# Four parts of w_in ahead of the attention loop, between the first loads

## The chip, the core and the metric

The kernel runs on one NeuronCore of a Trainium2 chip. The metric is the time of one execution in device microseconds (us). Its engines are TensorE (PE, with its weight loads listed as PEld), VectorE (DVE), ScalarE (ACT) and GpSimd (POOL); SyncE (SP) issues nearly all transfers. Each engine runs its own instructions strictly in order and waits on semaphores for the others.

## What is computed

Three stages follow each other. The first is attention over 512 local positions with a window of 32 either way, plus 32 global positions, for 4 batches and 8 heads of 64. The second is a dense feed-forward layer on its 2,176 tokens, and the third a routed layer of eight experts.

```
x = attention(q_l, k_l, v_l, q_g, k_g, v_g)            # 2176 x 512
h = x @ w_in                                           # 512 -> 2048
g = max(h, 0) + alpha * min(h, 0)
y = g @ w_out                                          # 2048 -> 512
# then each token goes to one of 8 experts with 272 places each, the largest
# gate logits y @ w_gate first; out = max(y @ w1[e], 0) @ w2[e]
```

## The kernel before

**Attention** works on 16 units (a batch and two heads), two units to a *pair*: 8 pairs. `load(p)` (lines 323 to 335) issues a pair's loads, one transfer for queries and keys (`qk`, line 332) and one for values (`v`, line 335) per unit. The first pair's `qk` comes in two cuts, one of 416 columns and one of 1,024, so that products can start early. There are four `qk` and four `v` buffers, two pairs' worth. A pair has four *blocks* of 128 queries: scores on PE (line 366), mask and maximum on DVE (372), four exps on ACT (374), `norm` on DVE (379, 380, and four multiplications at 386), transposes (392, copied by ACT at 394), and products with the values (403, copied by ACT at 405). The global queries of a pair add lines 419 to 454. `attention()` is a generator; each `next` writes out a piece of this.

**Weights** `w_in` and `w_out` come in eight-byte floats and are worked out on the chip in *parts*: eight of `w_in` (`win_part`, parts 0 to 7) and eight of `w_out` (`wout_part`) for the first half of the hidden columns. `decode` (75 to 89) loads a part of 512 KB with a transfer on SP into `raw` (line 79, three buffers), takes the absolute value on ACT into `mag` (line 82, two buffers), and assembles the float in four steps on DVE (lines 83, 85, 86, 87). `split` (71 to 73) then casts the high part on ACT (line 72) and subtracts it for the low part on POOL (line 73).

**The dense layer** goes over the tokens in column blocks of 272; its first product (`gemm1`, line 172) needs `w_in`'s parts, its leaky relu is an ACT step (177) and a DVE step that writes `g` (178), `g` is split (ACT and POOL, `ghi` and `glo`), and the second product (line 203) needs `w_out`'s parts. A first column block cannot be finished before the last part of `w_out` is there.

**Order.** Up to line 527, attention runs alone, until the first two pairs are done (`done[0]`), and after every sixth piece one of `w_in`'s parts 0 to 3 is written out. Lines 528 to 530 load `alpha` and the gate weights `wg`. Then a loop mixes attention with the dense layer and writes out one of the remaining twelve parts at each step of the latter, none of them issued ahead of the second pair's last norm. What the program writes out is reordered per engine by a scheduler before it runs, so the place in the code isn't the place in the queue: parts 0 to 3 stand in the queues behind much of the first pair.

Of the kernel before, what the change touches and what calls it, by code (L numbers as in the profile page):

```python
# [25 lines left out]
def tile_attention_moe_moe(ctx: ExitStack, tc: tile.TileContext, qkw, vw,  # L26
# [5 lines left out]
    E, _, FF = w1.shape  # L32
# [4 lines left out]
    KD = DM // 128  # L37
# [14 lines left out]
    def kpos(i):  # L52
        return WIN * (i + (i + 1) // 2)
# [17 lines left out]
    def split(hi, lo, src, lo_eng=None):  # L71
        a = A.copy(hi, src)  # L72
        return a, (lo_eng or V).tensor_tensor(lo, src, hi.bitcast(F32), op=OP.subtract)  # L73
# [3 lines left out]
    def decode(pool, src, n):  # L77
        raw = pool.tile([128, n, 2], I32, name="raw", bufs=RB[0])
        nc.sync.dma_start(out=raw.rearrange("p n t -> p (n t)"), in_=src)
        low, high = raw[:, :, 0], raw[:, :, 1]  # L80
        mag = pool.tile([128, n], F32, name="mag", bufs=2)
        A.activation(out=mag, in_=high.bitcast(F32), func=AF.Abs)
        V.tensor_scalar(mag, mag, F64_MIN, None, op0=OP.max)
        bits = mag.bitcast(I32)
        V.tensor_scalar(bits, bits, 3, 0x3FFFFFF8, op0=OP.logical_shift_left, op1=OP.bitwise_and)
        V.scalar_tensor_tensor(bits, high, -0x40000000, bits, op0=OP.bitwise_and, op1=OP.bitwise_or)
        V.scalar_tensor_tensor(bits, low, 29, bits, op0=OP.logical_shift_right, op1=OP.bitwise_or)
        return mag
# [11 lines left out]
    def win_part(pool, hf, i):  # L100
        c, k = divmod(i, KD)
        o = hf * HF + c * 512
        val = decode(pool, w_in.bitcast(I32)[k * 128:(k + 1) * 128, 2 * o:2 * o + 1024], 512)
        split(WI[hf][:, 0, k, c * 512:(c + 1) * 512], WI[hf][:, 1, k, c * 512:(c + 1) * 512], val, lo_eng=P)
# [185 lines left out]
    with ExitStack() as at:  # L290
# [5 lines left out]
        dc = at.enter_context(tc.tile_pool(name="dc", bufs=1, side="right"))  # L296
# [23 lines left out]
        QS = 4 * WIN  # L320
        STEPS = S // QS

        def load(p):
            for cut in range(2 if p == 0 else 1):
                for u in (2 * p, 2 * p + 1):
                    d = U[u]
                    if not cut:
                        d["qk"] = ld.tile([128, S + KL + 2 * SG], F32, name="qk")
                        d["k"] = d["qk"][:, QS:QS + KL]
                        d["g"] = d["qk"][:, S + KL:]  # L330
                    part = slice(None) if p else (slice(0, QS + kpos(6)), slice(QS + kpos(6), None))[cut]
                    nc.sync.dma_start(out=d["qk"][:, part], in_=qkw[u, :, part])
            for u in (2 * p, 2 * p + 1):
                U[u]["v"] = ld.tile([128, NQ, 2 * D], F32, name="vv")
                nc.sync.dma_start(out=U[u]["v"].rearrange("p i d -> p (i d)"), in_=vw[u])
# [131 lines left out]
        def attention():  # L467
            todo = []

            def one():  # L470
                if todo:
                    x, f = todo.pop(0)
                    f()
                    yield x

            N = STEPS * NU // 2
            for n in range(N + 2):
                p, j = divmod(n, STEPS)
                if n < N:
                    if j == 0 and 2 * p + 2 < NU:  # L480
                        load(p + 1)
                    scores(p, j)
                    yield 0.75
                if 1 <= n <= N:
                    a_ = divmod(n - 1, STEPS)
                    norm(*a_)
                    ptrans(*a_)
                    yield 0.45
                yield from one()
                if n >= 2:  # L490
                    v, j2 = divmod(n - 2, STEPS)
                    pv(v, j2)
                    yield 1.0
                    if j2 == STEPS - 1:
                        gout(v)
                        yield 0.1
                if n < N and j == 0:
                    todo += [(0.8, lambda p=p: (gscores(p, 0), gscores(p, 1))), (0.0, lambda p=p: gnorm(p)),
                             (0.6, lambda p=p: (gtrans(p, 0), gtrans(p, 1))), (1.2, lambda p=p: gpv(p))]

        load(0)
        mask = mk.tile([128, 3, KW], F32, name="mask")
        P.memset(mask, 0.0)
        for h in range(4):
# [11 lines left out]
        gpat = mk.tile([128, KL], F32, name="gpat")  # L516
        P.memset(gpat, 0.0)
        UPB = H // 2
        parts = [(win_part, i) for i in range(2 * KD)]
        att = attention()  # L520
        n = 0
        while done[0] < UPB - 1:
            next(att)
            n += 1
            if n >= 6 and n % 6 == 0 and len(parts) > KD:
                f, i = parts.pop(0)
                f(dc, 0, i)
        nc.sync.dma_start(out=al, in_=alpha.rearrange("(f p) -> p f", p=128))
        V.tensor_scalar(al1, al, -1.0, 1.0, op0=OP.mult, op1=OP.add)
        nc.sync.dma_start(out=wg[:, :, :E], in_=w_gate.rearrange("(k p) e -> p k e", p=128))  # L530
# [11 lines left out]
        while going:  # L542
# [12 lines left out]
            else:  # L555
# [4 lines left out]
                else:  # L560
                    spent["g"] += x
                    if parts:
                        f, i = parts.pop(0)
# [7 lines left out]
    with tc.tile_pool(name="dc2", bufs=1, side="right") as dc, tc.tile_pool(name="pW", bufs=2, space=PSUM) as pW:  # L571
        more = []
        parts = [(win_part, i) for i in range(2 * KD)] + [(wout_part, i) for i in range(KH)]
        n = 0
        while c < NCH:
# [4 lines left out]
            while next(g, None) is not None:  # L580
                n += 1
                if n % 5 == 0 and parts:
                    f, i = parts.pop(0)
# [13 lines left out]
    with ExitStack() as mo:  # L597
# [592 lines left out]
        for k in range(E):  # L1190
            n = 0.0
# [94 lines left out]
```

## Time and profile before

| | |
|---|---|
| median of 3 runs | 869.96 us (869.75 to 871.96) |
| profiled execution | 870.56 us, its span 868.8 us |
| mean granted clock of PE | 0.978 of full speed |
| PE busy | 820.1 us, 94% of the span |
| DVE busy | 466.8 us, 54% |
| ACT busy | 389.6 us, 45% |
| POOL busy | 348.5 us, 40% |

The span is the stretch from the first to the last instruction on the core; the execution's time has some 1.8 us around it. The shares are means over the whole span; the rows further down take it apart by stretch. In a row of the timeline, the first number is the start in us from the span's beginning, the second the time to the end of the last of the instructions that it groups (x4 stands for four in a row); brackets hold the engine's idle time just before and what released it. "PEclk" is PE's granted clock, where 1.00 stands for 2.4 GHz and 0.50 for 1.2.

### The profile page before, as it was taken

What the parts mean: (1) busy time and instruction counts of PE and PEld (TensorE: products, weight loads), DVE (VectorE), ACT (ScalarE), POOL (GpSimd) and SP (SyncE); (2) the same over time, 40 slices, a digit from 0 to 9 for tenths busy, and PEclk for the clock granted to TensorE, in tenths of its full rate; (3) what the DMA queues carried; (4) which work ended last, traced back from release to release, by engine and by line L of the source; (5) the groups of instructions that cost most, each with busy time, mean ns of one, the idle gap of its engine ahead of it and who ended that gap; (6) DMA issues with size and microseconds to landing.
All of it is one profiled execution on the core that took longest, in us unless ns stands there. A gap on an engine that the chain in (4) does not pass through costs nothing. (4 is left out here: it accounts for less than half of the span.)

```text
span 868.8 us, 21017 instructions
## 1 busy us (share of the span) xinstructions
PE 820.1 (94%) x8380; PEld 746.0 (86%) x8380; DVE 466.8 (54%) x1654; ACT 389.6 (45%) x970; POOL 348.5 (40%) x300
## 2 busy tenths in 40 slices
PE   6699799999988999999999999999899999999995
PEld 4478688888988999988898899999699989999995
DVE  4789945463288734133333457666575776722120
ACT  5577646464454543232322434341254535444431
POOL 1214412020145534200000638470598868779601
PEclk9589999999999999999999999999999999999998
DMA  9777715631345302201311217242366655666300
GB/s 345 230 255 272 261 38 192 212 124 47 95 134 183 114 26 79 72 7 53 103 52 54 78 54 267 64 131 65 100 198 217 168 177 153 174 187 185 111 25 37
DMA packets 50441, 115.94 MB, mean 133 GB/s; under 512 B 6759, under 2 KB 23399, under 8 KB 48295
## 3 DMA queue, kind: packets, MB, share of 16 engines
q1 hardware_dynamic: 47447, 105.68, 37.8%
q0 software_dynamic: 2896, 8.92, 3.1%
q8 instruction: 66, 1.08, 0.5%
q14 instruction: 32, 0.26, 0.1%
HBM read 96.76 MB, written 17.83 MB: 132 GB/s over the span
## 5 line engine op out<-in xcount | busy, mean ns | idle before, releaser
L172 PE MATMUL h<-xh,win 128*128 128x272 f32 x768 | 162.3, 295 | 3.9 <-DVE g L178 2.5
L73 POOL TENSOR_TENSOR m<-raw,m 128x1024 fp32r<-128x1024 f32 x64 | 152.4, 2402 | 21.6 <-ACT m L72 21.3
L172 PEld LDWEIGHTS h<-xh,win 128*128 128x128 f32 x768 | 124.9, 188 | 12.0 <-issue 4.9
L73 POOL TENSOR_TENSOR glo<-g,ghi 128x272 fp32r<-128x272 f32 x64 | 55.4, 866 | 150.8 <-ACT ghi L72 150.7
L203 PE MATMUL y<-ghi,wout 128*128 128x272 f32 x512 | 112.5, 298 | 2.5 <-ACT wout L72 1.3
L172 PE MATMUL h<-xl,win 128*128 128x272 f32 x384 | 111.3, 290 | 1.4 <-DVE xl L73 1.4
L1104 PE MATMUL h<-gr,wout 128*128 128x272 f32 x768 | 110.7, 295 | 0.0
L73 POOL TENSOR_TENSOR gr<-gb,gr 128x272 fp32r<-128x272 f32 x64 | 48.0, 772 | 153.2 <-ACT gr L72 144.6
L977 PE MATMUL h<-xsh,m 128*128 128x272 f32 x512 | 107.4, 297 | 1.3 <-ACT xsh L72 1.3
L993 PE MATMUL h<-hh,m 128*128 128x272 f32 x512 | 103.2, 293 | 0.0
L1104 PEld LDWEIGHTS h<-gr,wout 128*128 128x128 f32 x768 | 99.2, 188 | 0.9 <-ACT gr L72 0.4
L203 PEld LDWEIGHTS y<-ghi,wout 128*128 128x128 f32 x512 | 84.3, 188 | 8.3 <-issue 4.0
L177 ACT ACTIVATE neg<-h 128x272 f32<-128x272 f32 x128 | 50.5, 395 | 90.1 <-PE h L172 89.7
L977 PEld LDWEIGHTS h<-xsh,m 128*128 128x128 f32 x512 | 83.1, 190 | 1.9 <-ACT xsh L72 1.4
L993 PEld LDWEIGHTS h<-hh,m 128*128 128x128 f32 x512 | 81.7, 188 | 0.7 <-issue 0.5
L72 ACT CAST m<-raw 128x1024 fp32r<-128x1024 f32 x64 | 65.4, 1049 | 29.1 <-DMA raw<-in_moe_w_dram 28.9
L993 PE MATMUL h<-hl,m 128*128 128x272 f32 x256 | 75.5, 295 | 0.0
L203 PE MATMUL y<-glo,wout 128*128 128x272 f32 x256 | 73.8, 293 | 1.8 <-POOL glo L73 1.5
L977 PE MATMUL h<-xsl,m 128*128 128x272 f32 x256 | 74.9, 292 | 0.5 <-DVE xsl L73 0.5
L172 PEld LDWEIGHTS h<-xl,win 128*128 128x128 f32 x384 | 72.3, 188 | 2.4 <-DVE xl L73 1.9
L178 DVE SCALAR_TENSOR_TENSOR gb<-neg,al,h 128x272 f32<-128x272 f32 x64 | 31.6, 496 | 76.5 <-ACT neg L177 66.0
L374 ACT ACTIVATE pr<-sc,mx 128x128 f32<-128x128 f32 x128 | 50.1, 393 | 30.6 <-DVE mx L372 30.4
(231 smaller groups left out, 1517.2 us busy)
## 6 DMA issues: line engine op xcount, KB each, us to landing
raw<-in_moe_w_dram SPq DMA_DIRECT2D x64, 512.0 KB, 3.8
vv<-in_v_dram SPq DMA_DIRECT2D x16, 1024.0 KB, 8.0
qk<-in_qk_dram SPq DMA_DIRECT2D x14, 720.0 KB, 8.5
raw<-in_moe_w_in_dram SPq DMA_DIRECT2D x16, 512.0 KB, 4.4
raw<-in_moe_w_out_dram SPq DMA_DIRECT2D x16, 512.0 KB, 4.2
xs<-xb SPq DMA_DIRECT2D x16, 272.0 KB, 8.8
xpart<-xd SPq DMA_DIRECT2D x32, 136.0 KB, 1.7
xb<-xs SPq DMA_DIRECT2D x8, 544.0 KB, 4.0
```

The costliest lines, as they stand in the source:

```text
L72: a = A.copy(hi, src)
L73: return a, (lo_eng or V).tensor_tensor(lo, src, hi.bitcast(F32), op=OP.subtract)
L172: T.matmul(ps, wi[:, w, k, fs], x[:, k], start=i == 0, stop=i == 3 * KD - 1)
L177: A.activation(out=neg, in_=ps, func=AF.Relu, scale=-1.0)
L178: epi[0] = V.scalar_tensor_tensor(g, neg, al1[:, hf * KH + f:hf * KH + f + 1], ps, op0=OP.mult, op1=OP.add)
L203: T.matmul(ps, wo[:, w, f, ds_], x[:, f], start=i == 0, stop=i == 3 * KH - 1)
L374: A.activation(out=d["pr", j][:, ii], in_=sc, func=AF.Exp, bias=d["mx", j][:, ii:ii + 1], scale=-1.0, accum_out=d["sm", j][:, ii:ii + 1])
L977: T.matmul(ps, d["w1"][:, w, kk, fs], x[:, kk], start=i == 0, stop=i == 3 * KD - 1)
L993: T.matmul(ps, d["w2"][:, w, f, ms], x[:, f], start=i == 0, stop=i == 3 * K3 - 1)
L1104: T.matmul(ps[j], wo[:, w, f, ds_], x, start=f == 0 and a == 0, stop=f == KH - 1 and a == 2)
```

## The change

Parts 0 to 3 of `w_in` are no longer written out by the loop of lines 519 to 527 but inside the first `load`: parts 0 and 1 behind the first cuts of `qk`, parts 2 and 3 behind the second cuts, ahead of the values. Whatever belongs to a part (its transfer, ACT, DVE and POOL instructions) is written out there. The remaining parts keep their places in the code.

```
-        def load(p):
+        def load(p, between=()):
             for cut in range(2 if p == 0 else 1):
                 for u in (2 * p, 2 * p + 1):
...
                     nc.sync.dma_start(out=d["qk"][:, part], in_=qkw[u, :, part])
+                for f in between[2 * cut:2 * cut + 2]:
+                    f()
...
-        load(0)
+        parts = [(win_part, i) for i in range(2 * KD)]
+        load(0, [lambda i=i: win_part(dc, 0, i) for _, i in parts[:KD]])
+        del parts[:KD]
...
-        parts = [(win_part, i) for i in range(2 * KD)]
         att = attention()
-        n = 0
         while done[0] < UPB - 1:
             next(att)
-            n += 1
-            if n >= 6 and n % 6 == 0 and len(parts) > KD:
-                f, i = parts.pop(0)
-                f(dc, 0, i)
```

What the scheduler makes of it is seen in the engines' queues. In the following rows the line numbers after the change are two higher inside `load` from the values on and in attention, and two lower behind the loop.

SyncE's queue from its first transfer, before (`qk` and `vv` are attention's loads, `raw` a part, `al` and `wg` the alpha and the gate weights; x2 is one for each unit of a pair):

```order
L332 DMA qk<-in_qk_dram 128x416 x2
L332 DMA qk<-in_qk_dram 128x1024 x2
L335 DMA vv<-in_v_dram 128x2048 x2
L332 DMA qk<-in_qk_dram 128x1440 x2
L335 DMA vv<-in_v_dram 128x2048 x2
L79 DMA raw<-in_moe_w_in_dram 128x1024 x3
L528 DMA al<-in_moe_alpha_dram 128x16x1
L530 DMA wg<-in_moe_w_gate_dram 128x4x8
```

The same queue after:

```order
L332 DMA qk<-in_qk_dram 128x416 x2
L79 DMA raw<-in_moe_w_in_dram 128x1024 x2
L332 DMA qk<-in_qk_dram 128x1024 x2
L79 DMA raw<-in_moe_w_in_dram 128x1024
L337 DMA vv<-in_v_dram 128x2048 x2
L332 DMA qk<-in_qk_dram 128x1440 x2
L337 DMA vv<-in_v_dram 128x2048 x2
L526 DMA al<-in_moe_alpha_dram 128x16x1
L528 DMA wg<-in_moe_w_gate_dram 128x4x8
L79 DMA raw<-in_moe_w_in_dram 128x1024 x3
```

Two parts now stand ahead of the first pair's second cuts and one behind them; the fourth needs a `raw` buffer that the first has left, and it stands behind the gate weights.

ACT's queue before, from its second row (`pr` exps, `pt` and `gt` copies of transposes, `gsc` the global exps, `xb` the output copies, `mag` a part's absolute value):

```order
L374 ACTIVATE pr,sm<-sc,mx 128x128 x8
L394 COPY pt<-t 128x512
L424 ACTIVATE gsc,gmx<-gsc,gmx 128x544
...
L443 COPY gt<-gt 128x512
L374 ACTIVATE pr,sm<-sc,mx 128x128
L82 ACTIVATE mag<-raw 128x512
```

And after, its first rows, then the fourth part and what stands around it:

```order
L82 ACTIVATE mag<-raw 128x512
L376 ACTIVATE pr,sm<-sc,mx 128x128 x4
L82 ACTIVATE mag<-raw 128x512
L72 CAST win<-mag 128x512
...
L376 ACTIVATE pr,sm<-sc,mx 128x128 x4
L82 ACTIVATE mag<-raw 128x512
L407 COPY xb<-o 128x2x128
L396 COPY pt<-t 128x512
L82 ACTIVATE mag<-raw 128x512
L72 CAST win<-mag 128x512
L82 ACTIVATE mag<-raw 128x512
L407 COPY xb<-o 128x2x128
```

The first part's absolute value is now ACT's first instruction, and the fourth to sixth stand between the exps of the second pair's first and second blocks.

GpSimd's queue from the first subtract on, before (`win` and `wout` are the low parts of weights, `glo` that of one leaky relu):

```order
L73 TENSOR_TENSOR win<-mag,win 128x512 x8
L73 TENSOR_TENSOR glo<-g,ghi 128x272 x3
L73 TENSOR_TENSOR wout<-mag,wout 128x512
L73 TENSOR_TENSOR glo<-g,ghi 128x272
L73 TENSOR_TENSOR wout<-mag,wout 128x512
L73 TENSOR_TENSOR glo<-g,ghi 128x272 x2
L73 TENSOR_TENSOR wout<-mag,wout 128x512
L73 TENSOR_TENSOR glo<-g,ghi 128x272
```

And after:

```order
L73 TENSOR_TENSOR win<-mag,win 128x512 x8
L73 TENSOR_TENSOR wout<-mag,wout 128x512 x2
L73 TENSOR_TENSOR glo<-g,ghi 128x272
L73 TENSOR_TENSOR wout<-mag,wout 128x512 x2
L73 TENSOR_TENSOR glo<-g,ghi 128x272 x2
L73 TENSOR_TENSOR wout<-mag,wout 128x512
L73 TENSOR_TENSOR glo<-g,ghi 128x272
L73 TENSOR_TENSOR wout<-mag,wout 128x512
```

The parts of `w_out` have moved ahead against the leaky relus: before, two stand ahead of the sixth `glo`, after, seven.

## Rows read from the trace of the kernel before

**Rows 1.** Busy us by stretch: start:end and length first, (x) instructions, clock, DMA
```profile
core 0: us, PE busy (x) PEld busy (x) DVE busy (x) ACT busy (x) POOL busy (x), PEclk, DMA share, GB/s
5.10:24.50 19.40, 15.88 (x274) 10.37 (x274) 11.02 (x73) 10.08 (x41) 0.00 (x0) 1.00 1.01 403
24.50:39.70 15.20, 7.43 (x104) 4.38 (x105) 12.40 (x31) 8.27 (x20) 3.81 (x3) 0.54 0.71 217
39.70:50.50 10.80, 10.70 (x160) 7.80 (x160) 6.35 (x39) 8.45 (x32) 1.26 (x1) 0.54 0.84 268
50.50:85.20 34.70, 32.34 (x565) 26.53 (x548) 33.58 (x116) 26.24 (x83) 12.75 (x11) 1.00 0.74 264
85.20:112.00 26.80, 21.52 (x293) 17.43 (x297) 26.15 (x77) 17.93 (x51) 11.09 (x9) 1.00 0.62 215
112.00:200.00 88.00, 88.00 (x1411) 76.82 (x1398) 45.77 (x230) 50.96 (x179) 13.99 (x17) 1.00 0.40 139
```

**Rows 2.** Timeline at 25 us: start, duration, engine, line, op, [idle before <-releaser]
```profile
24.56 0.66 ACT L82 ACTIVATE mag<-raw 128x512 f32<-128x512 f32 x1 [2.19 <-DMA raw<-in_moe_w_in_dram]
27.23 1.92 PE L403 MATMUL o<-pt,vv 128*64 128x32 f32 x32 [2.78 <-ACT xb L405]
28.02 0.62 ACT L72 CAST win<-mag 128x512 fp32r<-128x512 f32 x1 [0.84 <-DVE mag L87]
```

**Rows 3.** Busy times of a short stretch, columns as in rows 1
```profile
48.00:50.00 2.00, 2.00 (x20) 0.85 (x24) 0.02 (x1) 1.17 (x4) 0.00 (x0) 0.60 0.89 254
```

**Rows 4.** SyncE's queue, timeline: start of issue, time held
```profile
7.49 4.14 SPq L79 DMA_DIRECT2D raw<-in_moe_w_in_dram  x3
16.62 10.20 SPq L530 DMA_DIRECT2D wg<-in_moe_w_gate_dram  x1
```

**Rows 5.** Issue to landing, line 79's transfers up to 130 us
```profile
DMA to landing us min/median/max: 3.5/4.5/17.0
```

**Rows 6.** Timeline before 46 us: first exp, waiting product, two norms
```profile
5.41 0.40 ACT L374 ACTIVATE pr<-sc,mx 128x128 f32<-128x128 f32 x1 [3.38 <-DVE mx L372]
7.52 0.65 PE L366 MATMUL s<-qk 64*32 64x128 f32 x8 [2.59 <-DMA qk<-in_qk_dram]
28.38 1.90 DVE L386 TENSOR_SCALAR pr<-pr,sm 128x128 f32<-128x128 f32 x4
41.99 0.87 DVE L386 TENSOR_SCALAR pr<-pr,sm 128x128 f32<-128x128 f32 x4
```

**Rows 7.** Timeline of VectorE: two steps of a decode without company
```profile
25.71 0.43 DVE L85 TENSOR_SCALAR mag<-mag 128x512 int32<-128x512 int32 x1
26.17 0.69 DVE L86 SCALAR_TENSOR_TENSOR mag<-raw,mag 128x512 int32<-128x512 int32 x1
```

**Rows 8.** VectorE's groups, 50.5 to 85.3 us: xcount | busy us, mean ns
```profile
L386 DVE TENSOR_SCALAR pr<-pr,sm 128x128 f32<-128x128 f32 x18 | 6.1, 393 | 0.1
L86 DVE SCALAR_TENSOR_TENSOR mag<-raw,mag 128x512 int32<-128x512 int32 x7 | 5.9, 865 | 0.0
L87 DVE SCALAR_TENSOR_TENSOR mag<-raw,mag 128x512 int32<-128x512 int32 x7 | 4.7, 677 | 0.0
L85 DVE TENSOR_SCALAR mag<-mag 128x512 int32<-128x512 int32 x7 | 4.6, 684 | 0.1
L83 DVE TENSOR_SCALAR mag<-mag 128x512 f32<-128x512 f32 x7 | 2.8, 420 | 0.4 <-ACT mag L82 0.4
```

**Rows 9.** Timeline at 78 us: GpSimd's subtract beside a decode step
```profile
77.44 1.27 POOL L73 TENSOR_TENSOR wout<-mag,wout 128x512 fp32r<-128x512 f32 x1 [0.54 <-ACT wout L72]
77.74 1.52 DVE L86 SCALAR_TENSOR_TENSOR mag<-raw,mag 128x512 int32<-128x512 int32 x1
```

**Rows 10.** Timeline: the three marks of the reckoning
```profile
50.54 0.29 DVE L372 CUSTOM_DVE_ANT_0 sc<-s,mask 128x128 f32<-128x128 f32 x1
84.74 0.48 DVE L178 SCALAR_TENSOR_TENSOR g<-neg,al,h 128x272 f32<-128x272 f32 x1
110.99 1.41 POOL L73 TENSOR_TENSOR wout<-mag,wout 128x512 fp32r<-128x512 f32 x1 [3.61 <-ACT wout L72]
```

## The prediction, made before the changed kernel ran

> **What bounds the kernel now.** I read the busy times by stretch first, since the mean share of an engine hides four regimes in the first 112 us [rows 1]. Up to 24.5 us the transfers set the pace: 403 GB/s, while VectorE (DVE) is busy for 11.02 of 19.40 us, so it has 8.4 us to spare. From 24.5 to 39.7 TensorE (PE) works only 7.43 of 15.20 us, and from there to 50.5 it is full (10.70 of 10.80), both at a granted clock of 0.54, about the lower of its two levels. From 50.5 DVE is the bound (33.58 of 34.70, then 26.15 of 26.80), with the clock whole. From 112 us PE is full (88.00 of 88.00). So whatever the time is at 112 us passes through to the end.
>
> The timeline shows where the second regime starts. ScalarE (ACT) stands at 24.56 us on an encoded part, the exps of the second pair queue behind it, and PE waits 2.78 us for an ACT copy [rows 2]. After that the clock is halved; it is back between 48 and 50 us, where the slice reads 0.60 and the next ones 1.00 [rows 3], some 9.8 us after the stretch in which PE stopped pausing began (39.7).
>
> I reckon with three marks [rows 10]: M1, the third pair's first score on DVE (50.54); M2, the end of the sixth leaky relu of the first column block (84.74 + 0.48 = 85.22); M3, GpSimd's last subtract for w_out (110.99), just ahead of the stretch where PE is full.
>
> **The change part by part: up to M1.** The first four parts leave the loop and go into the first load; their work is unchanged, so only its place counts. SyncE's order places two transfers ahead of the second cuts of the first pair and one behind them; the fourth stands behind the gate weights.
>
> *Later start.* A part and a second cut are both 512 KB, so the first part lands where the second cut's first half did, about 7.5 us [rows 6]; ACT now has its Abs ahead of all exps. The first exp goes from 5.41 to about 8.1: 2.7 us late. The second cuts come two places, 2 x 0.52 MB at 403 GB/s = 2.6 us, later.
>
> *Parts in the gap.* Before, three parts were issued from 7.49 us on [rows 4] but ACT came to the first only at 24.56. Alone, a decode on DVE is 0.42 + 0.43 + 0.69 + 0.68 = 2.22 us [rows 7, 8]. Three parts are 6.7 us, inside the 8.4 spare. So the norm of the second pair's first block, no longer delayed by a part on ACT, comes about where it was, 28.4 [rows 6], with three parts done rather than some 1.3.
>
> *The stall again.* SyncE is held by the gate weights, whose place in the bytes is the same, from 16.62 to 26.82 [rows 4]. The fourth part is issued then and lands at the soonest 3.5 us later [rows 5]: 30.4. Its Abs stands on ACT ahead of a copy that PE needs, so PE idles from about 28.7 to 31.4. Then a chain: Abs 0.66 to 31.1, decode 2.24, cast 0.62, GpSimd's subtract 1.27 [rows 9] (the sixth part's buffer waits for it), Abs 0.66, copy 0.35, four exps of 0.40: 38.0, and with the norm's two small steps 38.4, against 41.99 [rows 6]: a lead of 3.6.
>
> *To M1.* Behind that norm no decode is left, only PE's 10.70 us of work at half clock. If the clock stayed low, M1 is 38.4 + 10.7 = 49.1; if it returns about 10 us after PE runs on (some 33, so 43), the 4.6 us to there leave 6.1 x 0.54 = 3.3: M1 at 46.4. With no stall, DVE's work sets it: 12.40 + 6.35 [rows 1], less two decodes, from 28.4, so 42.6. I take 46.4, since no decode of DVE's stands in that stretch: **-4.1 us, bounds -7.9 and -1.4.**
>
> **From M1 to M2.** In DVE's order 6.7 decodes stand between M1 and M2 before and 11.2 after, 4.45 more; on GpSimd seven subtracts for w_out, not two, stand ahead of the sixth low half of g. Here a decode's four steps measure 0.42 + 0.68 + 0.87 + 0.68 = 2.65 us [rows 8], beside GpSimd's work: 4.45 x 2.65 = +11.8. DVE has no room (33.58 of 34.70), so all of it is on the path. Norms run at 0.39 against 0.22 alone [rows 6, 8]; with the subtracts crowded here, I add 1.3. Less 2.3 for what is done ahead of M1 now (a norm 0.87, three decode steps 2 x 0.42 + 0.43, small steps 0.2); plus 1.0 for landings, whose median is 4.5 us [rows 5], where three buffers now cycle faster: **+11.8, bounds +7.6 (the price alone, 4.45 x 2.22 = 9.9, less 2.3) and +15.2 (2.5 more for the lock of rival D, 0.9 more for landings).**
>
> On the price: a decode step that began 0.30 us into a subtract of 1.27 took 1.52 us, not 0.69, so it lost 0.83 of the 0.97 that the subtract had left [rows 7, 9]; over the stage a part loses only 2.65 - 2.22 = 0.43. The Trainium skill ("SBUF — State Buffer", section "Who interferes with whom") has it that VectorE and GpSimd share a pair of ports, which the one that starts first holds for its whole instruction. The one row agrees; were every subtract to hold off VectorE from start to end, the sum would be 2.5 us higher.
>
> **From M2 to M3.** The last decodes have moved ahead of M2. PE works 21.52 of 26.80 us here [rows 1]; its 5.3 us of waiting, for DVE and for ACT's casts of w_out, can go, and six products of the second matmul now stand ahead (about 0.5): PE-bound at 21.1. **-5.7, bounds -6.0 (a little more) and -3.4 (waits on attention's norms stay).**
>
> **Sum.** -4.1 + 11.8 - 5.7 = +2.0 us at M3, from where PE carries it on. The profiled execution took 870.56 us (span 868.8, so 1.8 around it), 0.6 over the median of 869.96. So 872.6 on the profiled one, **872.0 us** against the median. It is a difference of large terms: DVE gains some 6.7 us of filled idle time at the start and loses it to a late start, a new wait, and a tail where PE, not DVE, sets the pace.
>
> **The rivals.**
> *A, the clock stays low up to M1.* For it: before, half clock lasted until PE had run on for 9.8 us, and here PE starts with a wait for the fourth part. Against: fewer waits follow. It decides if the clock has not returned by about 46 us. M1 at 49.1 gives -1.4 + 11.8 - 5.7 = +4.7: 874.7, slower.
>
> *B, no second stall.* If the gate weights hold SyncE less long, so that the fourth part is issued before about 23 us, ACT finds it there, PE does not pause and the clock stays whole: M1 at 42.6, -7.9 + 11.8 - 5.7 = -1.8: 868.2. Against: the same transfers stand ahead of the gate weights as before.
>
> *C, the lead carries through.* As B, and the extra decodes cost the price alone, since GpSimd's subtracts meet DVE's reads of PSUM: -7.9 + 7.6 - 5.7 = -6.0: 864. For it: two of the four steps show no loss here (0.42 and 0.68) [rows 8]. Against: DVE and GpSimd are both at their densest there.
>
> *D, a full lock.* Each subtract stops DVE for its whole 1.27 us [rows 9]: 4.45 x 1.27 = 5.7 in place of the 4.45 x 0.43 + 1.3 = 3.2 counted: +2.5 more, 874.5, slower. For it: the row in which 0.83 of 0.97 was lost. Against: two of the four steps lost nothing in the stage [rows 8]. This is the rule of the Trainium skill's page named above.
>
> *E, the change does nothing*, were the parts late in the queue as before; SyncE's order excludes it.
>
> **How the numbers follow.** A measurement of this kernel can tell about 0.3% from no change: 867.35 to 872.57. The forecast has 0.38, of it 0.30 within 0.3% and 0.08 slower, since 872.0 is near the bound. A has 0.22 and D 0.08, slower. B has 0.18, 0.11 within and 0.07 faster. C has 0.14, faster. Faster 0.21, same 0.41, slower 0.38. The range takes in the forecast's near bounds, most of A, D and B: 867.0 to 876.5, leaving out C and the worst of M1 to M2 with A. Both signs hold weight, so the likeliest one's own range is 870.0 to 873.5.
>
> **What would show it.** The first exp near 8.1 us; a norm near 28.4 with three casts of w_in done before it; ACT waiting for line 79's transfer near 30, and PE idle 2 to 3 us ahead of it; a clock of about 0.5 from 31 to 43; M1 at 46.4, M2 at 92.9, M3 at 114.0 with PE full from M2. Wrong would be: the clock at 1.00 through 30 to 45 (B or C), M1 after 48 (A), M1 to M2 under 43 us (C) or over 49 (D), or PE still pausing over 2 us in all after M2.

## The result, and the profile after

The changed kernel takes 0.71% longer: the ratio to the kernel before is 1.0071, 95% interval 1.0056 to 1.0087, with medians of 876.8 us (7 runs, 874.3 to 878.4) against 870.2 us. By the ratio that is some 876.1 on the 869.96 of the prediction. It lies inside the range given (867.0 to 876.5), close to its upper end, and 4 us above the forecast of 872.0, on the side that had a chance of 0.38; the narrower range given for the likeliest outcome, 870.0 to 873.5, leaves it out. The profiled execution took 876.11 us, its span 874.2.

The busy times in the same stretches as [rows 1], changed kernel (columns as there):

```profile
5.10:24.50 19.40, 10.87 (x146) 6.42 (x147) 16.61 (x70) 10.61 (x37) 3.91 (x3) 0.89 1.01 404
24.50:39.70 15.20, 12.66 (x234) 8.95 (x232) 7.36 (x37) 8.51 (x29) 1.27 (x1) 0.80 0.81 248
39.70:50.50 10.80, 7.41 (x151) 5.59 (x143) 6.73 (x41) 7.37 (x28) 0.00 (x0) 0.87 0.57 184
50.50:85.20 34.70, 24.85 (x380) 19.04 (x381) 34.34 (x96) 22.93 (x67) 12.69 (x10) 0.79 0.75 263
85.20:112.00 26.80, 24.53 (x390) 20.92 (x387) 23.58 (x82) 18.49 (x58) 11.37 (x10) 0.94 0.40 142
112.00:200.00 88.00, 88.00 (x1361) 76.75 (x1359) 43.64 (x226) 49.74 (x176) 11.77 (x14) 1.00 0.48 166
```

DVE is busier at the start (16.61 of 19.40 us, before 11.02) and idler in the middle: 14.09 of the 26 us from 24.5 to 50.5, where it was 18.75. The work pulled forward has left a hole there. PE is busy for 5.0 us less in the first stretch, 3.3 less in the third and 7.5 less in the fourth, for 5.2 more in the second and 3.0 more in the fifth. From 98 us on DVE is no longer full, while PE is.

The start and the stall, changed kernel, timeline of ACT and PE (bracket: idle before, and what ended it):

```profile
7.30 0.66 ACT L82 ACTIVATE mag<-raw 128x512 f32<-128x512 f32 x1 [5.27 <-DMA raw<-in_moe_w_in_dram]
10.50 0.65 PE L368 MATMUL s<-qk 64*32 64x128 f32 x8 [5.48 <-DMA qk<-in_qk_dram]
18.56 0.81 PE L368 MATMUL s<-qk 64*32 64x128 f32 x26 [2.33 <-DVE mx L374]
32.84 0.66 ACT L82 ACTIVATE mag<-raw 128x512 f32<-128x512 f32 x1 [3.10 <-DMA raw<-in_moe_w_in_dram]
33.81 1.75 PE L405 MATMUL o<-pt,vv 128*64 128x32 f32 x32 [2.28 <-ACT xb L407]
```

ACT's first instruction is now the first part's absolute value, at 7.30. PE waits 5.48 us for the second cuts (before 2.59, [rows 6]) and 2.33 for DVE, and a stall like the one for the first part before [rows 2] comes 8 us later, for the fourth part: ACT waits 3.10 us, PE 2.28.

SyncE's queue, and the landing times of the parts' transfers up to 40 us:

```profile
13.06 13.48 SPq L528 DMA_DIRECT2D wg<-in_moe_w_gate_dram  x1
26.65 1.39 SPq L79 DMA_DIRECT2D raw<-in_moe_w_in_dram  x3
28.13 1.44 SPq L332 DMA_DIRECT2D qk<-in_qk_dram  x2
```

```profile
DMA to landing us min/median/max: 4.5/6.8/9.4
```

The three marks and the norms that lead to them, on DVE (answers to [rows 6] and [rows 10]):

```profile
30.19 0.88 DVE L388 TENSOR_SCALAR pr<-pr,sm 128x128 f32<-128x128 f32 x4
40.84 0.87 DVE L388 TENSOR_SCALAR pr<-pr,sm 128x128 f32<-128x128 f32 x4
49.97 0.68 DVE L388 TENSOR_SCALAR pr<-pr,sm 128x128 f32<-128x128 f32 x3
51.09 0.76 DVE L83 TENSOR_SCALAR mag<-mag 128x512 f32<-128x512 f32 x2
52.10 0.29 DVE L374 CUSTOM_DVE_ANT_0 sc<-s,mask 128x128 f32<-128x128 f32 x1
...
97.81 0.48 DVE L178 SCALAR_TENSOR_TENSOR g<-neg,al,h 128x272 f32<-128x272 f32 x1
```

M1 is at 52.10 us (before 50.54) and M2 at 98.29 (85.22). M3, GpSimd's last subtract for `w_out`, came at 101.26 (110.99): the decodes end early now, and it no longer marks where PE runs full. A fourth mark shows what passes on to the end: the fifth pair's first score on DVE, at 112.16 before and 118.47 after. Over the kernels of this study, the profiled execution's time less this mark is 756 to 760 us for all fourteen, so what a kernel gains or loses is settled there. The mark, before and after, and the busy times up to it:

```profile
112.16 0.29 DVE L372 CUSTOM_DVE_ANT_0 sc<-s,mask 128x128 f32<-128x128 f32 x1 [0.57 <-PE s L366]
118.47 0.29 DVE L374 CUSTOM_DVE_ANT_0 sc<-s,mask 128x128 f32<-128x128 f32 x1 [3.19 <-PE s L368]
0.00:112.16 112.16, 89.67 (x1415) 67.39 (x1415) 89.93 (x335) 72.25 (x227) 32.93 (x45) 0.89 0.75 264
0.00:118.47 118.47, 88.51 (x1415) 67.64 (x1416) 91.09 (x335) 72.40 (x228) 33.09 (x45) 0.87 0.71 252
```

Up to the mark PE runs 1,415 products in both. They keep it busy for 88.5 us, before 89.7, so its work at a lower clock is not what the change costs. It stands idle for 30.0 us, before 22.5, and these 7.5 us more of waiting are the loss.

**Where the time went.** M1 to M2 took 46.2 us instead of 34.7. Its worst part is the first 16 us. Changed kernel, then the kernel before:

```profile
52.10:67.80 15.70, 7.92 (x135) 4.86 (x132) 15.48 (x41) 8.98 (x22) 5.57 (x4) 0.69 0.68 240
```

```profile
50.54:67.00 16.46, 15.47 (x276) 12.02 (x266) 16.04 (x67) 12.42 (x42) 3.33 (x2) 1.00 0.68 245
```

DVE is full in both, but PE is busy for 7.92 us against 15.47. The timeline of the changed kernel there, some rows in order of time, with the dense layer's first product of the kernel before as the last row:

```profile
54.48 1.29 DVE L87 SCALAR_TENSOR_TENSOR mag<-raw,mag 128x512 int32<-128x512 int32 x2
55.90 2.51 POOL L73 TENSOR_TENSOR win<-mag,win 128x512 fp32r<-128x512 f32 x2 [18.02 <-ACT win L72]
56.10 2.78 DVE L388 TENSOR_SCALAR pr<-pr,sm 128x128 f32<-128x128 f32 x4
59.71 0.69 DVE L86 SCALAR_TENSOR_TENSOR mag<-raw,mag 128x512 int32<-128x512 int32 x1
61.59 0.22 DVE L456 COPY xb<-go 128x64 f32<-128x64 f32 x1
61.87 1.97 PE L421 MATMUL gs<-qk 128*64 128x512 f32 x4 [2.42 <-DVE xb L456]
62.44 1.65 DVE L87 SCALAR_TENSOR_TENSOR mag<-raw,mag 128x512 int32<-128x512 int32 x1
65.34 1.35 DVE L83 TENSOR_SCALAR mag<-mag 128x512 f32<-128x512 f32 x1
67.81 0.56 PE L172 MATMUL h<-xh,win 128*128 128x272 f32 x1 [1.76 <-DVE mx L374]
58.31 0.52 PE L172 MATMUL h<-xh,win 128*128 128x272 f32 x2
```

DVE has decodes in its queue ahead of small attention steps. In the 16 us behind M1 it runs 16 decode steps in both kernels, but between M1 and the 0.22 us copy at 61.59 eleven of them stand now, before seven, and only four multiplications of norms come in these 16 us, before ten. PE waits 2.42 us for that copy, 1.44 and 1.78 for copies of ACT, then 1.76 for a score's maximum, and the first product of the dense layer starts at 67.81 us, before at 58.31.

Four multiplications of a norm take 2.78 us, not 0.87 [rows 6], while two subtracts of GpSimd run. One by one they last 1.16, 1.31, 0.27 and 0.28 us, and the two long ones end 0.09 and 0.08 us behind a subtract's end. The steps of decodes at 62.44 and 65.34 are long beside a subtract too. The Trainium skill's page "SBUF — State Buffer" (section "Who interferes with whom") tells of a shared pair of ports, which whichever of the two engines issues first holds for its whole instruction; the ends of these two multiplications agree with it.

From M2 to the fifth pair PE is full and DVE is not:

```profile
98.34:118.50 20.16, 20.16 (x291) 17.33 (x292) 12.60 (x58) 12.29 (x42) 4.62 (x4) 0.92 0.61 216
```

### The profile page after: what moved, and what is told of

It is laid out like the page before. It is cut to its first block, busy times and chain, and to the rows that moved or that the text cites. A ratio compares the mean times of both kernels' runs of the same rounds, so it can differ in the third digit from the quotient of the medians.

```text
span 874.2 us, 21025 instructions
## 1 busy us (share of the span) xinstructions
PE 819.0 (94%) x8380; PEld 747.4 (86%) x8380; DVE 467.4 (53%) x1654; ACT 390.6 (45%) x970; POOL 348.4 (40%) x300
## 4 chain that ended last, share of the span: by engine, by line
PE 70%; DVE 10%; issue 7%; ACT 4%; POOL 4%; DMA 4%; SPq 1%; POOLq 0%; ACTq 0%; DVEq 0%
PE h L172 21%; PE h L1102 12%; PE y L203 9%; PE h L991 7%; PE h L975 6%; PE o L405 2%; POOL m L73 2%; DMA raw<-in_moe_w_in_dram 2%; DVE mag L86 2%; PE lp L260 2%; DVE mag L87 1%; DMA raw<-in_moe_w_dram 1%; PE s L368 1%; DVE pr L388 1%; PE go L454 1%
## 5 line engine op out<-in xcount | busy, mean ns | idle before, releaser
L172 PE MATMUL h<-xh,win 128*128 128x272 f32 x768 | 166.4, 300 | 7.2 <-DVE g L178 4.2
L172 PEld LDWEIGHTS h<-xh,win 128*128 128x128 f32 x768 | 127.7, 192 | 15.9 <-issue 7.1
L177 ACT ACTIVATE neg<-h 128x272 f32<-128x272 f32 x128 | 50.5, 396 | 93.4 <-PE h L172 92.9
```

Of the source, the lines that this page charges most:

```text
L172: T.matmul(ps, wi[:, w, k, fs], x[:, k], start=i == 0, stop=i == 3 * KD - 1)
L177: A.activation(out=neg, in_=ps, func=AF.Relu, scale=-1.0)
```

## The experiments

All ratios are to the kernel before, in runs on the same chip. The table gives for each kernel M1, the end of the last decode (line 87), the fifth pair's first score (us, profiled execution), and PE's busy time in the 16 us after M1.

| kernel | ratio, 95% interval | M1 | last decode | fifth pair | PE in 16 us |
|---|---|---|---|---|---|
| before | 1 | 50.5 | 110.3 | 112.2 | 15.0 |
| changed | 1.0071 (1.0056 to 1.0087) | 52.1 | 100.5 | 118.5 | 8.2 |
| e1 gate weights late | 1.0073 (1.0050 to 1.0096) | 51.6 | 100.8 | 118.7 | 8.0 |
| e2 before, gate weights late | 1.0094 (1.0069 to 1.0118) | 53.7 | 118.0 | 119.9 | 16.0 |
| e3 decodes later | 1.0091 (1.0071 to 1.0110) | 52.1 | 112.7 | 121.7 | 10.1 |
| e4 behind the cuts | 0.9969 (0.9940 to 0.9998) | 48.0 | 108.3 | 108.6 | 15.5 |
| e5 loads only | 1.0037 (1.0014 to 1.0061) | 53.8 | 115.5 | 117.5 | 16.0 |
| e6 tie earlier | 1.0169 (1.0152 to 1.0187) | 64.8 | 85.3 | 127.2 | 11.7 |
| e7 cuts and tie | 1.0010 (0.9987 to 1.0034) | 44.4 | 100.2 | 112.2 | 15.0 |
| e8 cuts, alpha late | 0.9970 (0.9950 to 0.9990) | 45.2 | 108.8 | 110.1 | 16.0 |
| e9 behind the values | 1.0029 (1.0007 to 1.0050) | 51.2 | 112.3 | 114.3 | 16.0 |
| e10 gap filled | 1.0015 (0.9999 to 1.0031) | 47.7 | 109.3 | 111.4 | 16.0 |
| e11 cuts, filled | 1.0084 (1.0069 to 1.0099) | 49.2 | 105.6 | 117.5 | 13.9 |
| e12 before, filled | 1.0114 (1.0098 to 1.0130) | 48.6 | 106.3 | 118.2 | 14.5 |

The first theory was that the lead was lost in SyncE's queue (Q), the rivals that it was lost at the start (S) or to the crowding of decodes (C).

**e1, the gate weights held back.** The changed kernel, with

```
-        nc.sync.dma_start(out=wg[:, :, :E], in_=w_gate.rearrange("(k p) e -> p k e", p=128))
...
+    with tc.issue_after(sent[0].ins):
+        nc.sync.dma_start(out=wg[:, :, :E], in_=w_gate.rearrange("(k p) e -> p k e", p=128))
```

(`sent[0]` is attention's last output transfer.)

> The changed kernel, with the load of the gate weights held in SyncE's queue behind the last output transfer of attention; nothing else moves in that queue. Theory Q (the queue): the changed kernel lost its lead because the fourth part stands behind the gate weights, was issued at 26.65 us and landed at 32.84. Then the fourth part is issued by about 13 us here, lands before 22, the pause of 2.28 us that ends at 33.81 is gone, M1 comes at 46 to 48 rather than 52.1, and the time is 871 to 873 rather than 876. Theory S (the start): the loss comes from two parts ahead of the second cuts, which is unchanged here; M1 moves by less than 2 us and the time stays within 1.5 us of the changed kernel's.

No change: 1.0073. The queue stood no shorter, now in the parts' own issues behind alpha, and ACT found its part at 31.23 (SyncE, then ACT):

```profile
13.89 15.81 SPq L79 DMA_DIRECT2D raw<-in_moe_w_in_dram  x3
31.23 0.68 ACT L82 ACTIVATE mag<-raw 128x512 f32<-128x512 f32 x1 [1.49 <-DMA raw<-in_moe_w_in_dram]
```

M1 moved by 0.5 us. So the price of the wait was not put to the test here.

**e2, the same in the kernel before.**

> The control: the kernel before, with the load of the gate weights held back in the same way. Both theories expect 870 within 1.5 us: before, the fourth part waits for a buffer that the first leaves at about 28 us, not for SyncE's queue; the stall at 24.56 stays. If this gains over 2 us, the gate weights cost something by themselves, and what the first run gains says less about the change.

A miss by both theories: 0.94% slower. The queues of the engines hardly differ from those of the kernel before, but PE, full from 44 us on, stayed at half clock (granted 0.50, 1.2 GHz) to past 66:

```profile
44.00:66.00 22.00, 22.00 (x280) 16.04 (x280) 12.43 (x63) 11.05 (x38) 1.28 (x1) 0.50 0.69 237
```

Before, the clock was back by 50 us. Up to the fifth pair PE is idle as long as before (22.1 us, before 22.5) and busy for 97.9 us, before 89.7, with the same 1,415 products: here the loss is the clock. Why it stayed low here, with PE as full, no run shows.

**e3, decodes later.** The changed kernel, with

```
-                        with tc.issue_after(at_norm[UPB // 2 - 1, STEPS - 1].ins):
+                        with tc.issue_after((epi[0] if f is wout_part and epi[0] is not None else at_norm[UPB // 2 - 1, STEPS - 1]).ins):
                             f(dc, 0, i)
```

and a part of `w_out` only at every second step (`epi[0]` is the latest leaky relu).

> The changed kernel, with each part of w_out tied in VectorE's queue behind the latest leaky relu written out before it, so that three subtracts for w_out rather than seven stand ahead of the sixth low half (two in the kernel before). Theory C (crowding): the decodes ahead of the leaky relus cost what the changed kernel loses; M1 stays at 52, M1 to M2 falls from 46.2 us to 37 to 40, and the time falls by 3 to 5 us, to 871 to 873. Theory V (VectorE's work is only moved): M1 to M2 falls as much, but the stretch to where PE runs full grows by the same, and the time stays within 1.5 us of 876.

Neither: M2 came 4.4 us earlier (93.9), the fifth pair 3.2 later, and the time is 0.2% longer than the changed kernel's by the ratios. The ties act on `w_out`'s parts, but PE had starved before them (10.1 of 16 us), on the four parts of `w_in`. The crowding that counts is in the third pair, ahead of the place where I had priced it.

**e4, all four parts behind the second cuts.**

```
-                for f in between[2 * cut:2 * cut + 2]:
+                for f in between if cut else ():
                     f()
```

> The changed kernel, with all four parts behind the second cuts of the first pair and none between the cuts. Theory S: the second cuts land at about 7.5 and 8.8 us as before, PE's pause of 5.48 us before 10.50 falls to some 2.6, the granted clock does not fall at 20 us, the norm of the second pair's first block comes at 27 to 28.5 rather than 30.2, and the time falls by 2 to 4 us, to 872 to 874. Theory Q: the fourth part still stands behind the gate weights, so the stall is as late as before and the time stays within 1.5 us of 876.

The direction of theory S, and far more than it forecast: 1.0% less than the changed kernel, and 0.3% less than before (the interval just excludes no change). PE's first wait, two norms, M1, and PE in the 16 us behind it:

```profile
6.80 0.65 PE L368 MATMUL s<-qk 64*32 64x128 f32 x8 [1.96 <-DMA qk<-in_qk_dram]
30.46 0.87 DVE L388 TENSOR_SCALAR pr<-pr,sm 128x128 f32<-128x128 f32 x4
37.98 0.88 DVE L388 TENSOR_SCALAR pr<-pr,sm 128x128 f32<-128x128 f32 x4
47.97 0.29 DVE L374 CUSTOM_DVE_ANT_0 sc<-s,mask 128x128 f32<-128x128 f32 x1 [0.17 <-PE s L368]
48.00:64.00 16.00, 15.52 (x299) 12.34 (x283) 15.01 (x65) 12.89 (x43) 3.20 (x3) 0.94 0.68 230
```

The first wait is 1.96 us, M1 comes 4.1 us earlier. Two expectations missed: the clock still fell at 19 us, and the norm came at 30.46, as late as in the changed kernel. The lead arises between that norm and the next (37.98 against 40.84) and up to M1. So theory S has the place of the parts right, but not the steps; and the edit also changed the order further on, since 10.75 decodes stand ahead of the sixth leaky relu on DVE, as in the kernel before, where the changed kernel has 15.25, and PE no longer starves behind M1.

**e5, the transfers alone.** The change's transfers stay between the cuts, but the work on the parts is written out behind the first block's scores:

```
+                for i in between[2 * cut:2 * cut + 2 - cut]:
+                    fetch(dc, i)
...
+            if len(parts) > KD:
+                with tc.issue_after(exps[0].ins):
+                    for f, i in parts[:KD]:
+                        f(dc, 0, i)
```

> The changed kernel's transfers as they are (two parts between the first pair's cuts, one behind them), but the work on the parts is written out behind the first block's scores and tied in ScalarE's queue behind its last exp, so that no absolute value stands ahead of the first exps. GpSimd's order further on is then that of the kernel before. Theory L (late cuts): what the changed kernel loses at the start comes from the second cuts, which land at 10.5 us instead of 7.5; they do here too, so PE pauses over 5 us there and the time stays within 2 us of 876. Theory A (ScalarE's order): the loss comes from the absolute values ahead of the exps and what follows from them in the queues; then the first exp comes at 5.4, M1 at 47 to 49, and the time falls to 866 to 870 although the second cuts are as late.

In between: 1.0037, by the ratios 0.34% less than the changed kernel and 0.68% more than e4. The three differ in more than one thing, so these are not the prices of late cuts and of absolute values ahead of the exps. The first exp came at 5.46 us and PE went on at 10.28, as late as in the changed kernel. DVE's order of the decodes up to the sixth leaky relu is that of the kernel before here, and PE is full for the 16 us behind M1: the early transfers alone do not make it starve there. M1 is late all the same, with the clock at half level from 34.6 to 55.0 us. The runs spread from 870.1 to 880.3 us along with the granted clock: the five at 0.979 or more took up to 871.8, the six at 0.975 or less 875.0 and more. The profiled one is of the latter, so its M1 of 53.8 is not typical.

**e6 and e7, the tie of the later parts.** DVE's hole between 24.5 and 52 us might be the tie that keeps the fifth part behind the second pair's last norm. e6 is the changed kernel, e7 is e4, each with

```
-                        with tc.issue_after(at_norm[UPB // 2 - 1, STEPS - 1].ins):
+                        with tc.issue_after(at_norm[UPB // 2 - 1, 0].ins):
```

> The changed kernel, with the twelve later parts tied in VectorE's queue behind the second pair's first norm instead of its last. Theory M (the middle): the three parts decoded early only leave VectorE idle later, between 24.5 and 52 us, where it was busy for 14.1 us after and 18.8 before, since the fifth part cannot come ahead of the second pair's last norm; with the tie moved, two or more further parts are decoded by 52 us and the time falls by 3 us or more, to 873 or less. Rival: the transfers and ScalarE's waits for them, not the tie, keep VectorE idle there; parts ahead of exps stretch the second pair further, and the time is 875 or more.

> Both edits: the four parts behind the second cuts (866.8 in the run of that alone) and the twelve later ones tied behind the second pair's first norm. Theory M: the fifth and sixth part are decoded ahead of M1, and the time falls by 2 to 5 us, to 862 to 865. Rival as for the run with the tie alone: 867 or more.

That theory falls. More parts were decoded early (the last by 85.3 us in e6, before 110.3), and the time is 1.69% longer; e7 loses what e4 gained. M1 tells little of it: e7 has the earliest of all, 44.4, and no gain. Decodes done early aren't what the end waits for. Up to the fifth pair, e7's PE is idle for 4.4 us longer than e4's (20.3 against 15.9). In e6 PE is idle for less time than in the changed kernel (26.8 against 30.0 us), but busy for 100.5 us against 88.5 with the same 1,415 products, at a mean granted clock of 0.75 against 0.87: its further loss is the clock.

**e8, alpha late as well.** e4, with alpha's load behind the first pair's output transfers (`sent[0]` here) and the gate weights behind the last:

```
+        with tc.issue_after(sent[0].ins):
+            nc.sync.dma_start(out=al, in_=alpha.rearrange("(f p) -> p f", p=128))
```

> The four parts behind the second cuts, with the loads of alpha and of the gate weights both held back in SyncE's queue: alpha behind the first pair's output transfers, the gate weights behind the last ones. With the gate weights alone held back, the next transfer was held for 13.6 us instead (the queue stood from 15 to 29 us behind alpha, 2,048 pieces of 4 bytes). Theory H: alpha holds the queue; without it the fourth part is issued by 16 us and lands by 24, ScalarE's wait of 0.99 us at 31.7 is gone, and the time falls by 1 to 4 us, to 863 to 866. Rival: the fourth part is taken from the transfers' shared rate or from its buffer, or alpha collides later; the time is 866 or more.

Half of it: alpha did hold the queue. Without it the fourth and fifth part are issued from 13.20 us, and ACT takes both without a wait:

```profile
13.20 4.38 SPq L79 DMA_DIRECT2D raw<-in_moe_w_in_dram  x2
30.10 1.30 ACT L82 ACTIVATE mag<-raw 128x512 f32<-128x512 f32 x2
```

M1 comes 2.8 us earlier than in e4, yet the time is the same (0.9970 and 0.9969). The lead was lost at half clock, with PE full from 38.7 to 58.5 us:

```profile
38.70:58.50 19.80, 19.80 (x223) 13.28 (x223) 11.13 (x54) 11.44 (x39) 1.68 (x2) 0.50 0.73 237
```

So without the stall of the fourth part, the centre of my reckoning, no gain shows in the end. What the stall costs by itself stays open: e8 also moves the gate weights, which alone cost 0.94% in e2.

**e9, the parts behind the first pair's values.**

```
-                for f in between[2 * cut:2 * cut + 2]:
-                    f()
...
                 nc.sync.dma_start(out=U[u]["v"].rearrange("p i d -> p (i d)"), in_=vw[u])
+            for f in between:
+                f()
```

> The changed kernel with the four parts behind the first pair's values instead of between its cuts: cuts and values of the first pair keep their places, and the absolute values stand behind the first eight exps. Theory S (what counts is which of attention's transfers a part pushes back, and whether its absolute value stands ahead of exps): PE's waits for the second cuts (5.48 us in the changed kernel) and for the values (2.02 us with the parts behind the cuts) are both as short as before (2.6, none), the second pair's first norm comes by 27 us, and the time is 862 to 867. Rival R (any early part costs as much further on as it saves at the start, since the order behind it shifts): 869 to 874.

Nearer to the rival: 1.0029. But its reason isn't seen: DVE's order of the decodes up to the sixth leaky relu is that of the kernel before. PE waits only 1.21 us for the second cuts and not for values, yet M1 is at 51.2, with half clock from 18 to 49 us. Up to the fifth pair PE is idle for 6.4 us less than in the kernel before (16.1 against 22.5) and busy for 8.5 more (98.2 against 89.7): the clock took more than the waits gave.

**e10, the gap filled.** The changed kernel, with 40 products that are thrown away ahead of the first pair's second block of scores (tied behind the first block's):

```
+            if p == 0 and j == 1 and 40:
+                fill(s[0][:, 0], 40)
```

> The changed kernel with 40 extra products on PE, thrown away, tied between the scores of the first pair's first and second block, where PE stood still for 5.48 us. Theory K (the clock): the granted clock, at half level from 20.8 to 27 us in the changed kernel, stays whole up to 28 at least, the second pair's first norm comes 2 to 3 us earlier (27 to 28 us), M1 by 49, and the time falls by 3 us or more, to 873 or less. Rival: the order of the queues sets the pace there; the norm comes within 1 us of 30.2 and the time stays within 2 us of 876.

The time fell by 0.56%, to 1.0015, and M1 to 47.7, as theory K had it. But not by its steps: the clock fell all the same, at 22.0 us instead of 20.4, and the norm came at 30.92. The extra products changed the planned order too: the eighth subtract for `w_in` stands behind the first `glo` (x7, then one, where the change has x8), and PE starves no more behind M1. PE's and DVE's busy times at the start and behind M1:

```profile
5.10:24.50 19.40, 18.30 (x234) 14.84 (x241) 16.19 (x67) 9.86 (x34) 3.92 (x3) 0.93 1.02 402
47.70:63.70 16.00, 16.00 (x238) 11.92 (x228) 12.97 (x60) 11.63 (x40) 2.54 (x2) 0.79 0.77 274
```

The products themselves took 10.8 us of PE. So this run doesn't tell clock from order.

**e11 and e12, products ahead of transposes too.** e4 and the kernel before, each with 12 such products ahead of the second block and 6 ahead of each group of transposes of the first three pairs:

```
+            if p < 3 and 6:
+                fill(t[:, 0], 6)
```

> The four parts behind the second cuts (866.8 alone), with extra products on PE, thrown away: 12 ahead of the first pair's second block of scores and 6 ahead of each group of transposes of the first three pairs. Theory K: the clock stays whole where it was at half level, from 19 to 25 and from 39.8 to 49 us; PE's 9 us there shrink by some 4 and the time falls by 2 to 5 us, to 862 to 865, with less spread between runs. Rival: the extra products only take PE's time, or the queues' order shifts with them; 867 or more.

> The control for the filled runs: the kernel before with the same extra products (12 ahead of the second block of scores, 6 ahead of each group of transposes of the first three pairs). Theory K: ScalarE still stands on the first part at 24.5 us, so part of the pause stays, but the half clock from 26 to 49 us is shortened and the time falls by 1 to 4 us, to 866 to 869. Rival: 870 or more, as the pause itself, which the products don't fill since they stand ahead of it, brings the clock down.

Both are slower, 1.0084 and 1.0114, though the clock is better (mean 0.986, before 0.978). In e12 it was whole up to 34 us and again behind 48:

```profile
12.00:34.00 22.00, 21.15 (x411) 17.30 (x409) 16.66 (x77) 13.81 (x48) 2.54 (x2) 1.00 0.92 333
48.60:64.00 15.40, 13.89 (x218) 11.58 (x218) 14.35 (x49) 9.54 (x30) 2.63 (x2) 1.00 0.39 145
```

That doesn't refute theory K: up to the fifth pair the thrown-away products alone took 26.6 us of PE in e11 and 25.9 in e12, while PE's busy time grew by 11.1 us over e4 and 12.9 over the kernel before. What they cost by taking PE's time can hide what the clock gave. With the products in the queue the plan decodes early here too: the last decode ends 12 us ahead of the fifth pair.

**What the runs have in common.** In seven kernels the last decode ends within 2.1 us of the fifth pair's first score (before, e2, e4, e5, e8, e9, e10). In the other seven it ends 9 to 42 us earlier: the changed kernel, e1, e3, e6, e7, e11, e12. The two kinds differ in DVE's order: up to the sixth leaky relu, the first have 10.75 to 11.25 decodes, the second 11.75 to 16 (a step counts 0.25). Of the second kind none is faster than the kernel before and six of seven are 0.7% or more slower; of the first, only e2 is. That is a grouping over the runs; no run changed the order behind M1 alone with the success that e3 meant to have.

For the kernels without thrown-away products, PE's idle and busy time up to the fifth pair (profiled execution) says more, since they run nearly the same products up to there (1,404 to 1,430):

| kernel | decodes up to the sixth leaky relu | PE idle, us | PE busy, us |
|---|---|---|---|
| before | 10.75 | 22.5 | 89.7 |
| changed | 15.25 | 30.0 | 88.5 |
| e1 | 15.25 | 29.0 | 89.7 |
| e2 | 10.75 | 22.1 | 97.9 |
| e3 | 11.75 | 26.0 | 95.7 |
| e4 | 10.75 | 15.9 | 92.7 |
| e5 | 10.75 | 22.4 | 95.0 |
| e6 | 16.0 | 26.8 | 100.5 |
| e7 | 12.75 | 20.3 | 91.8 |
| e8 | 11.25 | 16.9 | 93.2 |
| e9 | 10.75 | 16.1 | 98.2 |

The changed kernel and e1 lose by waits, e2, e5 and e9 by the same work taking longer at half clock, e3 and e6 by both. That an order with more decodes ahead makes PE wait is what the traces show of the changed kernel; what brings the half clock in each of the others stays open. Nor is the half clock the same in every run of a kernel: e4's twelve runs go from 861.3 us at a mean granted clock of 0.983 to 873.3 at 0.967.

## Why the prediction was right in part

- **The range.** That the time lies in it is in part luck. The second and third terms of the sum came out near their forecasts, the first outside its own bounds, and the width of the range and what the third gave beyond its forecast took that up. The direction held; of the 6.2 us the forecast had 2.0.
- **Bounds of the kernel before.** Held: every kernel's gain or loss is settled by the fifth pair, and behind it PE is full.
- **Later start.** The first exp was expected at 8.1 us and came at 7.86; the second cuts at 10.1 and 11.4, and PE went on at 10.50. What I left out is what else that costs: PE waited 5.48 and then 2.33 us, the clock was at half level from 20.4 to 27.2 us, and the norm forecast for 28.4 came at 30.19.
- **The stall again.** Its place held: SyncE was held to 26.5 us, and PE paused. Its cause did only in part: without the gate weights the queue stands no shorter behind alpha (e1), without both it does not (e8). The transfer was under-priced: I took 3.5 us, the least of [rows 5], where 6.2 passed from 26.65 to 32.84, with two more parts and two 0.72 MB loads issued right behind it. The next norm came at 40.84, not 38.4.
- **M1, the step that failed.** Forecast 46.4 (-4.1, bounds -7.9 to -1.4), measured 52.10 (+1.6). The prediction let PE's work alone fill the time from the norm to M1: 8.0 us, of which 4.6 at half clock. It took 11.3 us. Rival A's reason isn't it, though its sign (M1 after 48) came: the clock was whole from 37.5 to 47.7 us. PE had waits there, 2.01 us for the next norm alone, and the third pair's first scores, whose products were done by 50.4 us, stand in DVE's order behind the second pair's last norm and three decode steps (the rows at 49.97 and 51.09 above). These 3.3 us and the 2.4 already lost at the norm make the 5.7 us. The bound of 42.6 for no stall was also too late as reckoned: it lets the 12.40 us of DVE's work, which begin at 24.5, begin at 28.4.
- **M1 to M2.** Forecast +11.8, measured +11.5. A decode's steps took 0.55 + 0.47 + 0.78 + 0.89 = 2.68 us, forecast 2.65; but a norm's multiplications took 0.68 each, where I had reckoned with little more than 0.39. One by one, undisturbed, they take 0.28; the 0.22 of the prediction is a fourth of four that overlap. VectorE's groups, M1 to M2:

```profile
L87 DVE SCALAR_TENSOR_TENSOR mag<-raw,mag 128x512 int32<-128x512 int32 x11 | 9.7, 889 | 0.0
L388 DVE TENSOR_SCALAR pr<-pr,sm 128x128 f32<-128x128 f32 x14 | 8.9, 680 | 0.0
L86 DVE SCALAR_TENSOR_TENSOR mag<-raw,mag 128x512 int32<-128x512 int32 x11 | 8.5, 775 | 0.1
L85 DVE TENSOR_SCALAR mag<-mag 128x512 int32<-128x512 int32 x12 | 5.7, 471 | 0.1
L83 DVE TENSOR_SCALAR mag<-mag 128x512 f32<-128x512 f32 x10 | 5.4, 545 | 0.1
```

  By these rows and [rows 8] the decode steps grew by 11.3 us and the multiplications by 2.8, though these are four fewer; the 1.0 us added for landings did not come, since DVE is idle for 0.4 us in this stretch, before 1.1. The sum was right; that PE would starve in the first 16 us of it was not seen.
- **M2 on.** Forecast -5.7, measured -6.8 up to the fifth pair (from +13.1 to +6.3) and -7.7 to the end of the span (+5.4). PE is full from M2, as forecast. The forecast of 114.0 for M3 goes by the end of the stretch, 112.0; from the 110.99 of its definition the same sum gives 113.0, and it came at 101.26.
- **The rivals.** The time is nearest to A and D (874.5 to 874.7), the mechanism is that of neither: for D, M1 to M2 would be over 49 us, and it is 46.2. B went by the stall: e8, which has none, comes to 867.4 by its ratio, near B's 868.2, but so does e4 (867.3), where ACT still waits for the fourth part. C went by the lead: e7 has one of 6 us at M1 and comes to 870.8, not 864.

## What to carry to other kernels

Work that is pulled forward into an engine's idle time is worth its place only if nothing on the way to the end is queued behind it; here its transfers stood ahead of the attention's own, its first step ahead of every exp, and moving it behind the second cuts, with the order that the planner then made, turned +0.7% into -0.3%. A lead at an early mark is no gain: compare kernels at the place where the bound changes over to the engine that keeps it to the end. Up to that place, read an engine's waits and its busy time apart, since a lower clock can take back what fewer waits give (e9). Where a planner orders the queues, read the order again behind each edit, since an edit at 5 us moved work at 55.

## What was not expected of the hardware

Alpha is 8 KB in pieces of 4 bytes. With its load and no gate weights behind it in the queue (e1), the issue of one 512 KB part held SyncE for 13.6 us; without it (e8), alpha itself took 9.6 us from issue to landing later on. And the granted clock came back at very different places with PE full: it was back by 50 us in the kernel before, and only past 66 us in e2, where PE had been full from 44 us on. What sets this stayed open.
